# Attention feeding two dense layers: k and q of eight items loaded four rows to a partition, and transposed one head at a time

## The chip, the cores and the metric

The kernel runs on one core of one Trainium2 chip. The metric is the device time of one execution in microseconds (us); three runs of the kernel before gave 863.14, 870.18 and 860.70 us, median 863.14.

## The reference, cut to what matters

```
q, k, v: (4, 8, 576, 64) fp32        # batch, heads, sequence, head width
q_d, k_d, v_d = mean over 4 neighbouring rows          # (4, 8, 144, 64)
out_d     = softmax(q_d k_d^T / 8) v_d, each row repeated 4 times
out_local = softmax(q k^T / 8 where |i - j| < 4) v
x   = (out_d + out_local), heads side by side          # (2304, 512)
h   = max(x w1, x w2, x w3);       x2  = h w_out        # 512 -> 768 -> 512
out = ((x2 w_a) * (x2 w_b)) w_out2                      # 512 -> 1536 -> 512
```

The weights arrive as 8-byte floats and are converted on the chip. Both attentions need q and k with the head width on the partitions, so each (576, 64) block has to be turned.

## The kernel before, in words

The 32 pairs of batch and head are taken as 16 *items* of two heads each. An item goes through steps that the code names by letters: `k` loads k and q (`a_load_qk`, L193), `v` loads v twice, once in rows of four for the pooled attention (`vr`, L223) and once in windows of 70 rows for the local one (`vw`, L231 and L233), `Q` turns k and q and pools them (`a_qk`, L249), `S` makes the scores and the softmax (`a_scores`), `T` turns the probabilities (`a_tr`) and `A` multiplies with v (`a_av`). All matmuls run on TensorE (PE); it writes PSUM banks, which VectorE (DVE) and ScalarE (ACT) read.

Items 0 to 7 are turned by TensorE and items 8 to 15 by VectorE's block transpose (`i >= TV`); only the first eight are touched by the change. For these, the tile `k` (or `q`) holds, in partition p, the rows p, 128 + p, 256 + p and 384 + p of both heads, 64 floats each (L211, one load a head), and the last 64 rows apart (L214). `a_qk` turns four pieces of 128 rows by 128 columns (both heads at once, L270) and the 64 last rows (L275). The turned k is copied to `kt` by ACT (L276), the turned q is summed over fours by DVE (L281) and copied to `qt` by ACT (L284). The pooled score is L306, the local one L323; `ps_ud` (L416) and `ps_av` (L431) are the products with v.

Beside the items, weights are loaded in pieces (`raw`, L475) and converted by DVE and ACT (L489 to L506), and products of the first dense layer (L624) fill TensorE where the attention leaves it free: from item 4 on, with lower priority. Behind the attention come the rest of the first layer (L624) and the second (L881), on TensorE almost without a break.

The order on each engine is made by a scheduler that takes the steps in the order of `PRE` and `LOOPS`, with priorities and its own idea of durations. All loads up to the second layer are issued by SyncE's queue (SP), in one line. Each takes one of eight counters in turn and waits until the load eight issues before it has landed; the rows of SP's order below show that as `DMAHW0` to `DMAHW7`.

Of the kernel before, what the change touches and what calls it, by code (L numbers as in the profile page):

```python
# [8 lines left out]
F32 = mybir.dt.float32  # L9
# [42 lines left out]
def attn_moe_kernel(  # L52
# [14 lines left out]
    nc = tc.nc  # L67
    B, H, S, D = q.shape
# [3 lines left out]
    P = 128  # L72
# [10 lines left out]
    RF = S // P  # L83
    RT = S - RF * P
# [25 lines left out]
    def bk(st, name):  # L110
        if 1 in psp_:
            return psp_[1].tile([P, 512], F32, tag="m", name=name)
        t, n = ("t", 3) if st in "tv" else ("m", 5)
        return psp_[0].tile([P, 512], F32, tag=t, name=name, bufs=n)
# [12 lines left out]
    ident = cst.tile([P, P], F32, name="ident")  # L127
# [11 lines left out]
    for t0, t1, q0 in ((0, NQ - 2, 1), (NQ - 2, NQ - 1, 0), (NQ - 1, NQ, NQ - 1)):  # L139
        off = q0 * QT - win(q0)  # L140
        for half in range(2):
            m = cap[half * 64 : half * 64 + 64, t0:t1, :]
# [34 lines left out]
    def pool(i, n):  # L177

        return ex if i < NI // 2 and i % n == n - 1 else ap_
# [12 lines left out]
    def a_load_qk(i):  # L192
        b, hp = items[i]  # L193
        s = st[i]
        h = 2 * hp
        engs = (nc.sync, nc.scalar if i < ACT_LOADS else nc.sync)
        if i >= TV:
            for nm, src in (("k", k), ("q", q)):
                x = pool(i, 2).tile([P, (RF + 1) * 2 * D], F32, tag=nm, bufs=1, name=nm)
                s[nm] = x[:, :S]  # L200
                for j in range(P // BS):
                    hh, d0 = divmod(j * BS, D)
                    nc.sync.dma_start(
                        x[j * BS : (j + 1) * BS, :S].rearrange("p (c d) -> p c d", d=BS),
                        src[b, h + hh, :, d0 : d0 + BS].rearrange("(c p) d -> p c d", p=BS),
                    )
            return
        for eng, nm, src in zip(engs, "kq", (k, q)):
            s[nm] = pool(i, 2).tile([P, RF + 1, 2, D], F32, tag=nm, bufs=1, name=nm)
            for j in range(2):  # L210
                eng.dma_start(  # L211
                    s[nm][:, :RF, j, :], src[b, h + j, : RF * P].rearrange("(r p) d -> p r d", p=P)
                )
            eng.dma_start(  # L214
                s[nm][:RT, RF], src[b, h : h + 2, RF * P :].rearrange("h p d -> p h d")
            )

    def a_load_v(i):
# [16 lines left out]
    def pool_qk(i, qp, n):  # L235
        s = st[i]
        s["kd"] = pool(i, 3).tile([P, SD], F32, tag="kd", bufs=1, name="kd")
        s["qd"] = qd[n]
        nc.vector.tensor_reduce(
            out=s["kd"], in_=s["kt"].rearrange("m (g f) -> m g f", f=FAC), axis=AX.X, op=ALU.add  # L240
        )
        for j in range(2):
            pj = slice(64 * j, 64 * j + 64)
            mark["q", i] = nc.scalar.mul(
                s["qd"][pj, :, j, :], qp[pj].rearrange("m (t i) -> m t i", t=NDQ), SCALE / (FAC * FAC)
            )
# [3 lines left out]
    def a_qk(i):  # L250
        s = st[i]
        n = i % 3 if i < NI // 2 else i % 2
        qt = s["qt"] = pool(i, 3).tile([P, S], F32, tag="qt", bufs=1 if pool(i, 3) is ex else 2, name="qt")
        s["kt"] = pool(i, 3).tile([P, S], F32, tag="kt", bufs=1 if pool(i, 3) is ex else 2, name="kt")
        NF = RF * P
        if i >= TV:
            nc.vector.transpose(s["kt"], s["k"])
            nc.vector.transpose(qt, s["q"])
            qp = ap_.tile([P, SD], F32, tag="qp", bufs=1, name="qp")
            nc.vector.tensor_reduce(  # L260
                out=qp, in_=qt.rearrange("m (g f) -> m g f", f=FAC), axis=AX.X, op=ALU.add
            )
            pool_qk(i, qp, n)
            return
        tail = bk("q", "ps_t2")
        pss = []
        for nm in ("k", "q"):
            ps = bk("q", "ps_t")
            for r in range(RF):
                nc.tensor.transpose(ps[:, r * P : (r + 1) * P], s[nm][:, r], ident)  # L270
            pss.append(ps)
        tails = []
        for m, nm in enumerate(("k", "q")):
            tails.append(tail[:, m * RT : (m + 1) * RT])
            nc.tensor.transpose(tails[m], s[nm][:RT, RF], ident[:RT, :RT])  # L275
        nc.scalar.copy(s["kt"][:, :NF], pss[0])  # L276
        nc.scalar.copy(s["kt"][:, NF:], tails[0])
        qp = ap_.tile([P, SD], F32, tag="qp", bufs=1, name="qp")
        for src, g0 in ((pss[1], 0), (tails[1], NF // FAC)):
            g1 = g0 + src.shape[1] // FAC  # L280
            nc.vector.tensor_reduce(  # L281
                out=qp[:, g0:g1], in_=src.rearrange("m (g f) -> m g f", f=FAC), axis=AX.X, op=ALU.add
            )
        nc.scalar.copy(qt[:, :NF], pss[1])  # L284
        nc.scalar.copy(qt[:, NF:], tails[1])
        pool_qk(i, qp, n)
# [740 lines left out]
    def emit(f, i):  # L1027
        if i < NI and (f, i) not in emitted:
            emitted.add((f, i))
            {"k": a_load_qk, "v": a_load_v, "Q": a_qk, "S": a_scores, "T": a_tr, "A": a_av}[f](i)  # L1030
# [9 lines left out]
    for i in range(NI):  # L1040
# [4 lines left out]
        for x in LOOPS.get(i, LOOP).split():  # L1045
            f, d = x[0], int(x[1:])
# [201 lines left out]
```

## Time and profile before

| | |
|---|---|
| runs, us | 863.14 (median), 860.70 to 870.18 |
| profiled execution, us | 869.63 |
| its span, first to last instruction, us | 867.9 |
| TensorE busy | 840.3 us, 97% |
| VectorE busy | 623.0 us, 72% |
| mean granted TensorE clock | 0.982 |

The profiled execution is 6.5 us above the median of the runs. TensorE's busy time is made of overlapping matmuls and says that it had something to do, not that it was at its peak; the engines' shares change from stage to stage, so the stages are read apart: up to 28 us, to 61 us, to 117 us and the rest.

### The profile page before, as it was taken

The numbers are of one execution on the slowest core, as the hardware profiler recorded it, in microseconds if no ns is written. First come the engines' busy times: TensorE is split into PE (matmuls) and PEld (weight loads), VectorE is DVE, ScalarE is ACT, GpSimd is POOL, SyncE is SP. The second block draws the span as 40 slices with busy tenths as digits, with TensorE's granted clock in tenths as the row PEclk, the third lists the DMA queues.
The fourth block names the chain that finished last, engine by engine and source line by source line (L and its number), as shares of the span: only waits on it lengthen the run. The fifth ranks groups of instructions, "written<-read, shape, count | busy, mean of one in ns | idle before, by whom it ended". The sixth has DMA issues, their size and how long they took to land.

```text
span 867.9 us, 14826 instructions
## 1 busy us (share of the span) xinstructions
PE 840.3 (97%) x5622; PEld 782.1 (90%) x5622; DVE 623.0 (72%) x1110; ACT 342.5 (39%) x771; POOL 368.0 (42%) x358
## 2 busy tenths in 40 slices
PE   5899889999999999999989999999999999999998
PEld 4777778999999999999989899999999899999997
DVE  5899976754575595776878899999999754234344
ACT  4685645554422231232335554434434432322211
POOL 4677655634232232242547564555554451111111
PEclk8799989999999999999999999999999999999999
DMA  8898833311111131240323545445443368666612
GB/s 188 176 197 134 153 89 84 75 36 41 58 64 49 37 100 35 73 158 26 134 98 136 181 181 182 172 169 182 172 168 129 127 214 305 233 218 218 242 48 73
DMA packets 125110, 116.22 MB, mean 134 GB/s; under 512 B 81392, under 2 KB 107760, under 8 KB 125040
## 3 DMA queue, kind: packets, MB, share of 16 engines
q1 hardware_dynamic: 120864, 98.51, 38.3%
q10 hardware_dynamic: 4176, 16.78, 5.4%
q8 instruction: 44, 0.72, 0.4%
q14 instruction: 26, 0.21, 0.1%
HBM read 80.66 MB, written 34.60 MB: 133 GB/s over the span
## 4 chain that ended last, share of the span: by engine, by line
PE 84%; DVE 7%; DMA 3%; issue 2%; SPq 1%; POOL 1%; ACT 1%; DVEq 0%; POOLq 0%
PE ps_m L624 48%; PE ps_u L881 28%; PE ps_av L431 2%; PE ps_tl L405 1%; DMA k<-in_k_dram 1%; PE ps_sd L306 1%; DMA vw<-in_v_dram 1%; PE ps_s L323 1%; DVE ce L499 1%; PE ps_td L395 1%; PE ps_ud L416 1%; PE ps_t L270 1%; DMA w<-y 1%; DVE cm L492 1%; DVE ce L489 0%
## 5 line engine op out<-in xcount | busy, mean ns | idle before, releaser
L624 PE MATMUL ps_m<-xh,w 128*128 128x384 f32 x864 | 174.4, 340 | 0.5 <-POOL w L512 0.4
L920 POOL TENSOR_TENSOR gl<-g,gh 128x384 fp32r<-128x384 f32 x72 | 78.2, 1086 | 183.3 <-ACT gh L919 153.7
L624 PEld LDWEIGHTS ps_m<-xh,w 128*128 128x128 f32 x864 | 151.7, 189 | 2.4 <-POOL w L512 0.7
L881 PE MATMUL ps_u<-xh,w 128*128 128x384 f32 x720 | 135.8, 338 | 0.1
L881 PEld LDWEIGHTS ps_u<-xh,w 128*128 128x128 f32 x720 | 128.1, 190 | 2.7 <-DVE t L653 0.4
L624 PE MATMUL ps_m<-wo,gh 128*128 128x512 f32 (+1 forms) x422 | 126.9, 393 | 1.2 <-DVE acc L989 1.2
L881 PE MATMUL ps_u<-xl,w 128*128 128x384 f32 x648 | 122.1, 336 | 0.7 <-ACT sn L893 0.7
L881 PEld LDWEIGHTS ps_u<-xl,w 128*128 128x128 f32 x648 | 113.9, 188 | 3.9 <-ACT sn L893 1.3
L893 ACT COPY sn<-ps_u 128x384 f32<-128x384 f32 x108 | 50.6, 478 | 119.6 <-PE ps_u L881 101.2
L624 PE MATMUL ps_m<-xl,w 128*128 128x384 f32 x432 | 94.5, 337 | 0.4 <-POOL xl L454 0.4
L989 DVE TENSOR_TENSOR acc<-ps_m,acc 128x512 f32<-128x512 f32 (+1 forms) x91 | 61.5, 680 | 42.6 <-PE ps_m L624 42.3
L653 DVE TENSOR_TENSOR t<-ps_m,t 128x384 f32<-128x384 f32 x72 | 39.9, 554 | 72.0 <-PE ps_m L624 64.8
L624 PEld LDWEIGHTS ps_m<-wo,gh 128*128 128x128 f32 x422 | 78.2, 188 | 14.5 <-DVE acc L989 1.6
L624 PEld LDWEIGHTS ps_m<-xl,w 128*128 128x128 f32 x432 | 76.5, 189 | 0.7 <-POOL xl L454 0.7
L624 PE MATMUL ps_m<-hh,wo 128*128 128x384 f32 x288 | 74.3, 337 | 2.4 <-DVE acc L680 2.4
L624 PE MATMUL ps_m<-wo,gl 128*128 128x512 f32 x211 | 66.4, 393 | 0.0
L659 POOL TENSOR_TENSOR hl<-t,hh 128x384 fp32r<-128x384 f32 x36 | 36.4, 1011 | 69.9 <-ACT hh L658 68.7
L919 ACT CAST gh<-g 128x384 fp32r<-128x384 f32 x72 | 37.1, 515 | 65.9 <-DVE g L910 62.0
L499 DVE SCALAR_TENSOR_TENSOR ce<-raw,ce 128x512 uint16<-128x512 uint16 x60 | 51.7, 862 | 15.8 <-ACT ce L496 15.8
L680 DVE TENSOR_TENSOR acc<-ps_m,acc 128x384 f32<-128x384 f32 x120 | 61.9, 552 | 1.1 <-PE ps_m L624 1.1
L496 ACT ACTIVATE ce<-ce,ebias 128x512 int16<-128x512 uint16 x60 | 43.4, 723 | 42.9 <-DVE ce L489 42.9
L812 POOL TENSOR_TENSOR w<-F,w 128x768 fp32r<-128x768 f32 (+1 forms) x36 | 56.3, 1580 | 5.2 <-ACT w L810 4.6
(127 smaller groups left out, 1369.7 us busy)
## 6 DMA issues: line engine op xcount, KB each, us to landing
dw<-w SPq DMA_DIRECT2D x24, 768.0 KB
raw<-in_moe_w_dram SPq DMA_DIRECT2D x18, 512.0 KB
raw<-in_moe_w_out_dram SPq DMA_DIRECT2D x18, 512.0 KB
w<-dw SPq DMA_DIRECT2D x12, 768.0 KB
w<-dw ACTq DMA_DIRECT2D x12, 768.0 KB
dw<-wo SPq DMA_DIRECT2D x12, 512.0 KB
wo<-dw ACTq DMA_DIRECT2D x11, 512.0 KB
vr<-in_v_dram SPq DMA_DIRECT2D x16, 288.0 KB
```

What stands on the lines that cost most here:

```text
L496: nc.scalar.activation(out=s16, in_=e, func=AF.Relu, bias=ebias, scale=8.0)
L499: nc.vector.scalar_tensor_tensor(out=e, in0=top, scalar=0x8000, in1=e, op0=ALU.bitwise_and, op1=ALU.bitwise_or)
L624: nc.tensor.matmul(ps, lhs[a], rhs[b], start=(i == 0), stop=(i == n - 1))
L653: nc.vector.tensor_tensor(out=t, in0=ps, in1=cur["t"], op=ALU.max)
L659: nc.gpsimd.tensor_tensor(out=l, in0=t, in1=h.bitcast(F32), op=ALU.subtract)
L680: nc.vector.tensor_tensor(out=a, in0=ps, in1=a, op=ALU.add)
L812: nc.gpsimd.tensor_tensor(out=l, in0=w, in1=h.bitcast(F32), op=ALU.subtract)
L881: nc.tensor.matmul(ps, w[:, a, slot, kk], y[:, b * HK + kk], start=start and i == 0, stop=i == 3 * HK - 1, skip_group_check=not start,)
L893: nc.scalar.copy(t, ps)
L919: nc.scalar.copy(h, g)
L920: nc.gpsimd.tensor_tensor(out=l, in0=g, in1=h.bitcast(F32), op=ALU.subtract)
L989: nc.vector.tensor_tensor(out=a, in0=ps, in1=a, op=ALU.add)
```

## The change

The tile keeps its size. Its first 512 columns now hold, for each head, four neighbouring rows of a partition (rows 4p to 4p + 3, 256 floats in one run), loaded for both heads by one DMA; the last 64 rows stay as they were. A tensor thus comes by two DMAs in place of three, and in runs of 1024 bytes in place of 256.

Since partition p now has rows 4p + r, the turned columns must land four apart: each piece goes to every fourth column of the PSUM bank. The four transposes of 128 columns (both heads) become eight matmuls of 64 columns (one head each) with the identity as the moving side, alternating between the lower and the upper 64 partitions of the output. They are ordinary matmuls, no longer transposes.

```diff
         for eng, nm, src in zip(engs, "kq", (k, q)):
-            s[nm] = pool(i, 2).tile([P, RF + 1, 2, D], F32, tag=nm, bufs=1, name=nm)
-            for j in range(2):
-                eng.dma_start(
-                    s[nm][:, :RF, j, :], src[b, h + j, : RF * P].rearrange("(r p) d -> p r d", p=P)
-                )
+            x = pool(i, 2).tile([P, (RF + 1) * 2 * D], F32, tag=nm, bufs=1, name=nm)
+            xr = x[:, : RF * 2 * D].rearrange("p (h r d) -> p h r d", h=2, r=RF)
+            xt = x[:RT, RF * 2 * D :]
+            s[nm] = xr, xt
             eng.dma_start(
-                s[nm][:RT, RF], src[b, h : h + 2, RF * P :].rearrange("h p d -> p h d")
+                xr.rearrange("p h r d -> p h (r d)"),
+                src[b, h : h + 2, : RF * P].rearrange("h (p r) d -> p h (r d)", r=RF),
+            )
+            eng.dma_start(
+                xt.rearrange("p (h d) -> p h d", h=2), src[b, h : h + 2, RF * P :].rearrange("h p d -> p h d")
             )
...
             for r in range(RF):
-                nc.tensor.transpose(ps[:, r * P : (r + 1) * P], s[nm][:, r], ident)
+                for j in range(2):
+                    pj = slice(64 * j, 64 * j + 64)
+                    nc.tensor.matmul(
+                        ps[pj].rearrange("m (p r) -> m r p", r=RF)[:, r],
+                        s[nm][0][:, j, r, :],
+                        ident,
+                        start=True,
+                        stop=True,
+                    )
...
-            nc.tensor.transpose(tails[m], s[nm][:RT, RF], ident[:RT, :RT])
+            nc.tensor.transpose(tails[m], s[nm][1], ident[:RT, :RT])
```

The scheduler orders the new program anew, and instructions move on every engine. Behind line 285 every line number is 12 higher in the changed kernel (L306 is L318 there), and the turning L270 is L276, its tail L275 is L287, the loads L211, L214, L223, L231 and L475 are L214, L218, L227, L235 and L487.

On SP, behind the loads of items 0 and 1, before (`k` and `q` are item 2's here):

```order
L475 DMA raw<-in_moe_w_dram 128x4x256
L211 DMA k<-in_k_dram 128x4x64 x2
L214 DMA k<-in_k_dram 64x2x64
L211 DMA q<-in_q_dram 128x4x64 x2
L214 DMA q<-in_q_dram 64x2x64
L475 DMA raw<-in_moe_w_dram 128x4x256
L223 DMA vr<-in_v_dram 72x4x256
L231 DMA vw<-in_v_dram 70x7x64
```

and now, with the counter that each load waits for:

```order
L487 DMA raw<-in_moe_w_dram 128x4x256 [waits DMAHW0_49]
L487 DMA raw<-in_moe_w_dram 128x4x256 [waits DMAHW1_49]
L227 DMA vr<-in_v_dram 72x4x256 [waits DMAHW2_49]
L235 DMA vw<-in_v_dram 70x7x64 [waits DMAHW3_49]
L237 DMA vw<-in_v_dram 70x2x64 [waits DMAHW4_49]
L214 DMA k<-in_k_dram 128x2x256 [waits DMAHW5_49,PE_49]
L218 DMA k<-in_k_dram 64x2x64 [waits DMAHW6_49]
L214 DMA q<-in_q_dram 128x2x256 [waits DMAHW7_49,PE_49]
L218 DMA q<-in_q_dram 64x2x64 [waits DMAHW0_49]
```

Item 2's loads stand behind two weight pieces and a part of item 0's v, where one weight piece stood ahead of them. Ahead of item 3's k there were 31 issues and are now 26, one of them the `vr` of a third item.

On TensorE, from item 0's local scores to the pooled scores of item 1, before:

```order
L323 MATMUL ps_s<-kt,qt 64x70 x18
L270 MATMUL ps_t<-ident,k 128x128 x4
L270 MATMUL ps_t<-ident,q 128x128 x4
L275 MATMUL ps_t_267<-ident,k 128x64
L275 MATMUL ps_t_267<-ident,q 128x64
L395 MATMUL ps_td<-ident,ed 72x96 x6
L270 MATMUL ps_t<-ident,k 128x128 x4
L270 MATMUL ps_t<-ident,q 128x128 x4
L275 MATMUL ps_t_308<-ident,k 128x64
L275 MATMUL ps_t_308<-ident,q 128x64
L306 MATMUL ps_sd<-kd,qd_93 96x144 x3
```

and now:

```order
L335 MATMUL ps_s<-kt,qt 64x70 x18
L276 MATMUL ps_t<-ident,k 64x128 x8
L276 MATMUL ps_t<-ident,q 64x128 x8
L287 MATMUL ps_t_269<-ident,k 128x64
L287 MATMUL ps_t_269<-ident,q 128x64
L407 MATMUL ps_td<-ident,ed 72x96
L276 MATMUL ps_t<-ident,k 64x128 x8
L276 MATMUL ps_t<-ident,q 64x128 x8
L287 MATMUL ps_t_316<-ident,k 128x64
L287 MATMUL ps_t_316<-ident,q 128x64
L407 MATMUL ps_td<-ident,ed 72x96 x5
L417 MATMUL ps_tl<-ident,el 70x128 x3
```

Eight matmuls stand where four transposes stood, and a part of item 0's turned probabilities (`ps_td`, `ps_tl`) now stands ahead of item 1's pooled scores.

On VectorE, from item 0's pooled k to the first sums of its probabilities, before:

```order
L239 TENSOR_REDUCE kd<-kt 128x144
L339 TENSOR_REDUCE md<-ps_sd 96x3
L489 TENSOR_SCALAR ce<-raw 128x512
L492 TENSOR_SCALAR cm<-raw 128x512
L497 SCALAR_TENSOR_TENSOR cm<-raw,cm 128x512
L363 TENSOR_REDUCE sd<-eps_138 96x3
```

and now:

```order
L243 TENSOR_REDUCE kd<-kt 128x144
L501 TENSOR_SCALAR ce<-raw 128x512
L504 TENSOR_SCALAR cm<-raw 128x512
L509 SCALAR_TENSOR_TENSOR cm<-raw,cm 128x512
L511 SCALAR_TENSOR_TENSOR ce<-raw,ce 128x512
L518 SCALAR_TENSOR_TENSOR cm<-cm,ce 128x512
L351 TENSOR_REDUCE md<-ps_sd 96x3
```

The whole conversion of the first weight piece stands ahead of item 0's first maximum (`md`), where it stood behind it.

## Rows read from the trace of the kernel before

**Rows 1.** The page, the span in 40 slices of 21.7 us, busy tenths.

```profile
PE   5899889999999999999989999999999999999998
DVE  5899976754575595776878899999999754234344
DMA  8898833311111131240323545445443368666612
```

**Rows 2.** Windows: length, busy us (instructions) of PE, PEld, DVE, ACT, POOL, PE clock, DMA, GB/s.

```profile
30.40:37.20 6.80, 6.80 (x70) 5.17 (x66) 5.17 (x11) 3.45 (x10) 5.17 (x6) 0.50 0.86 216
38.00:61.00 23.00, 21.91 (x303) 17.98 (x303) 21.94 (x63) 20.32 (x67) 18.43 (x20) 1.00 0.90 192
61.00:117.00 56.00, 49.51 (x593) 40.31 (x592) 55.80 (x114) 32.89 (x98) 34.76 (x38) 0.96 0.78 136
117.00:207.00 90.00, 90.00 (x965) 81.96 (x965) 53.29 (x140) 47.11 (x134) 44.22 (x54) 0.97 0.32 65
```

**Rows 3.** The chain of work that ended last, in order of time: start us, us, what.

```profile
13.53 6.13 DMA vw<-in_v_dram
...
22.16 6.36 DMA k<-in_k_dram
```

**Rows 4.** Timeline of PE to 29 us: start us, us, instructions, idle time before them and releaser.

```profile
4.33 1.09 PE L270 MATMUL ps_t<-ident,k 128*128 128x128 f32 x4 [4.33 <-DMA k<-in_k_dram]
...
15.49 0.69 PE L395 MATMUL ps_td<-ident,ed 96*72 96x96 f32 x6 [1.31 <-POOL ed L366]
...
20.72 1.75 PE L306 MATMUL ps_sd<-kd,qd 128*96 128x144 f32 x6 [1.50 <-DVE ce L499]
...
28.61 0.63 PE L270 MATMUL ps_t<-ident,k 128*128 128x128 f32 x4 [2.17 <-DMA k<-in_k_dram]
```

**Rows 5.** Timeline of PE from 50.6 to 55.3 us, nothing idle, clock 1.00.

```profile
50.62 0.66 PE L270 MATMUL ps_t<-ident,k 128*128 128x128 f32 x4
51.11 0.60 PE L270 MATMUL ps_t<-ident,q 128*128 128x128 f32 x4
...
52.58 0.72 PE L416 MATMUL ps_ud<-ptd,vd 72*64 72x144 f32 x8
53.23 0.98 PE L306 MATMUL ps_sd<-kd,qd 128*96 128x144 f32 x6
54.13 1.27 PE L431 MATMUL ps_av<-pt,vw 70*64 70x64 f32 x36
55.33 0.44 PE L395 MATMUL ps_td<-ident,ed 96*72 96x96 f32 x3
```

**Rows 6.** Timeline of SP's queue: start us, us, issues.

```profile
0.74 0.99 SPq L211 DMA_DIRECT2D k<-in_k_dram  x2
1.77 0.71 SPq L214 DMA_DIRECT2D k<-in_k_dram  x1
...
8.05 0.59 SPq L475 DMA_DIRECT2D raw<-in_moe_w_dram  x1
...
21.10 2.90 SPq L211 DMA_DIRECT2D k<-in_k_dram  x2
```

**Rows 7.** DMA from 4 to 7 us, k and q alone: packets, MB, share of 16 engines.

```profile
q1 hardware_dynamic: 2124, 0.52, 77.0%
```

**Rows 8.** DMA from 226 to 240 us, two weight pieces alone: packets, MB, share.

```profile
q1 hardware_dynamic: 1056, 1.05, 25.0%
```

**Rows 9.** Timeline of DVE around the first conversion.

```profile
10.64 0.60 DVE L339 TENSOR_REDUCE md<-ps_sd 96x3 f32<-96x432 f32 x1 [2.29 <-PE ps_sd L306]
12.34 0.43 DVE L489 TENSOR_SCALAR ce<-raw 128x512 uint16<-128x512 uint16 x1 [1.09 <-DMA raw<-in_moe_w_dram]
...
14.96 1.03 DVE L506 SCALAR_TENSOR_TENSOR cm<-cm,ce 128x512 f32<-128x512 f32 x1
```

**Rows 10.** Line L270 over the span: count, duration ns least/median/most, first and last start.

```profile
L270 PE MATMUL ps_t<-ident,k x32: 272/287/473, 4.3 to 58.5; 128*128 128x128 f32 x32
L270 PE MATMUL ps_t<-ident,q x32: 270/273/476, 5.7 to 59.7; 128*128 128x128 f32 x32
```

## The prediction

> **What bounds the kernel now.** I read the page's slices first [rows 1]: from the second slice on TensorE's digit is 8 or 9, while the DMA engines' is 8 or 9 only in the first five slices, some 108 us. All turning by L270 lies in the first 60 us, 64 instructions [rows 10], so the question is how these 60 us hand on to the rest. The windows then part the stages [rows 2]. From 38 to 61 us TensorE is busy 21.91 us of 23 and VectorE 21.94, at a granted clock of 1.00: both are full. From 61 to 117 us VectorE is full (55.80 of 56) and TensorE has 6.5 us left. From 117 us on TensorE is busy without a gap (90.00 of 90). What the first stages lose or win is therefore handed to the end, unless it fits into those 6.5 us.
>
> Before 28.6 us it is another picture. The chain of waits runs there through transfers, 6.13 us on a `vw` and 6.36 us on item 3's k [rows 3], and TensorE's timeline shows idle time: 4.33 us before the first k, 1.31 and 1.50 us on results of item 0 and 1, 2.17 us on item 3's k [rows 4].
>
> **The change, part by part.**
>
> *Turning, TensorE.* Now a tensor takes from 50.62 to 51.11 us, 0.49 us for four transposes [rows 5]. After it there are eight matmuls on 64 stationary columns. The rows show that an ordinary fp32 matmul is done as two: L306 stands three times in the program and six times in the trace [rows 5], so the eight are 16 passes of 128 columns. The nearest rows are L416 and L431, which also have 64 stationary columns and also go to the lower and upper half of the output in turn: 8 passes of 144 columns from 52.58 to 53.23 us (0.65 us), 36 passes of 64 columns from 54.13 to 55.33 us (1.20 us). With a fixed start s and c for a column of a pair of passes, s + 576c = 0.65 and s + 1152c = 1.20, so c = 0.955 ns and s = 0.10 us. Eight pairs of 128 columns: 0.10 + 8 x 128 x 0.000955 = 1.08 us. A tensor costs 0.59 us more.
>
> That is the value I take. From below: 16 passes in pairs cannot beat eight transposes of 128 columns, 8 x 0.49/4 = 0.98 us, 0.49 more. From above: L306, whose 96 columns leave no second half, takes 0.90 us for six passes of 144 columns [rows 5], 0.15 each; 16 x 0.15 x 128/144 = 2.13 us, 1.64 more. I take the paired rows because the pairing there is made by the same alternation of halves. In that sum the step of four in the output costs nothing; no row of this kernel has a matmul that writes PSUM with a step, so the dearer end stays in the range.
>
> Items 3 to 7 have ten such tensors, and from 28.6 to 61 us TensorE has no slack worth the name: 10 x 0.59 = 5.9 us on the path. Items 0 to 2 have six tensors, at the lower clock dearer (L270 at 4.33 us took 1.09 us in place of 0.66 [rows 4, 5]), some 0.6 to 1.2 us each. Item 0's lie on the path (about +1.1 us, its q being what the next step waits for); items 1 and 2 stand beside the waits of 1.31 and 1.50 us and are mostly covered by them. If those waits went, item 2's would cost about 2 us.
>
> *Loads.* A tensor's main part was 1024 packets of 256 bytes and is 256 of 1024. In 4 to 7 us, where only k and q run, 77.0% of 16 engines x 3 us for 2124 packets is 17.4 ns a packet [rows 7]; two weight pieces with 1024-byte rows took 25.0% of 16 x 14 us for 1056, 53 ns [rows 8]. Four times 17.4 is 69.6, so 16.6 ns are saved per 1024 bytes: 256 x 16.6 / 16 = 0.27 us of all engines per tensor, 4.2 us over 16 tensors. SP's issues fall by one a tensor, 16 in all at 0.5 us (two L211 took 0.99 us [rows 6]), 8 us of SP's time up to 54 us; and since each load waits for the one eight before it, fewer and larger ones keep more bytes under way. At 21.10 us two issues took 2.90 us [rows 6], held by that.
>
> What of it reaches TensorE: the 2.17 us wait on item 3's k. Its load has 26 issues ahead in place of 31, but among them a third `vr`. I take it as landing 0.5 to 2 us earlier; TensorE, held by item 0, comes there about 1.5 us later than 26.4 us. It starts item 3 near 28.0 in place of 28.6 us: -0.6 us. Behind that point loads don't end waits on TensorE until 61 us, so the rest of the saving is worth nothing there: both compute engines are full.
>
> *What is not touched.* The output's step restores the order of rows, so the readers L276, L281 and L284 and the tails L275 read what they read before. The order changes past 61 us hide among fills (L624) that are done sooner or later on an engine without gaps.
>
> *Sum.* -0.6 + 5.9 = +5.3 us at 61 us; of TensorE's 6.5 us of idle time to 117 us I let 1.3 take up some of it: **+4 us** at the end. On the profiled execution, 869.6 us, that is 873.6; it ran 6.5 us above the median of the runs, and I forecast the median: 863.1 + 4 = **867 us**.
>
> **The rivals.**
>
> *The turning runs at single pace (slower).* Place: the 16 passes of each tensor in `ps_t`. If the step of four in PSUM or the mode keeps them from pairing, a tensor costs 1.64 us more: items 3 to 7 +16.4; items 0 to 2 +9.8, of which the waits of 1.31, 1.50 and 2.17 us cover 5.0. 16.4 + 4.8 - 1.3 and some of VectorE's slack leave about +18: 881 us. It decides from about 1.0 us more a tensor on, where the ten reach 10 us. For it: nothing in the trace shows such a write to be free. Against it: an fp32 pass gives a column only every 0.9 ns or so, which leaves time for it. The Trainium skill ("PSUM — Partial Sum Buffer", Specifications) says that any non-contiguous access pattern slows matmuls significantly, without a figure; by that rule this rival is the outcome. No run here shows it yet.
>
> *Faster: loads and clock.* TensorE's clock was granted at 0.50 (1.2 GHz) from 30.4 to 37.2 us, 6.80 busy us [rows 2], right behind the idle 2.17 us. If item 3's k comes before TensorE asks and the clock stays at 2.4 GHz, 3.4 us come back, and the 2.17 us wholly: 5.9 - 2.2 - 3.4 - 1.3 = -1. If the earlier loads also take the first k's 4.33 us and the 1.31 and 1.50 us down by half, -3.6 more. About -3: 860 us, at best 852. For it: the chain names loads for 12.5 us of the first 28.5 [rows 3]. Against it: from 38 us no wait on loads is left to take.
>
> *The first conversion delays item 0.* VectorE's order now has the whole conversion ahead of `md`. It ran from 12.34 to 15.99 us, and `md` at 10.64 [rows 9]. With the weight piece issued near 6 in place of 8.05 us [rows 6], the conversion may end near 13.7, and item 0's softmax is 3 us late. Behind it TensorE waits with `ps_td`; 1 us is covered by item 3's wait: +2 on the forecast, 869 us.
>
> **How the numbers follow.** Forecast 0.48, single pace 0.18, faster 0.24, late conversion 0.10. The forecast's own range is 862 to 872: ends 0.49 to 0.8 us a tensor, and 3 us for the new order. The range of 8 in 10 takes in most of the faster case and half of the single pace: 856 to 879. One per cent, 8.6 us, is what a measurement of this kernel can tell from no change: the bounds are 854.5 and 871.8. Faster than that is a third of the faster case, 0.08; slower is the single pace and the tails of the forecast and the late conversion, 0.18 + 0.06 = 0.24; within it 0.68.
>
> **What would show it.** L276 (the turning) in rows of 16 per tensor, 1.0 to 1.1 us from the first to the next instruction at full clock: the first term. Near 2.1 us: single pace. In TensorE's timeline, item 3's k without a 2 us wait; clock near 1.00 in 30 to 37 us would speak for the faster case. The end of L440 and of VectorE's full stretch near 121 in place of 117 us: the hand-on. `md` of item 0 near 13.7 us: the late conversion. The forecast is wrong if the first 61 us become shorter, since that would mean that loads, not the two full engines, set their length.

## The result, and the profile after

The changed kernel takes 874.45 us (median of 4 runs, 873.79 to 876.46) beside 862.22 us of the kernel before (860.7 to 870.18): a ratio of **1.0122**, 95% interval 1.0093 to 1.0151. By that ratio, which isn't the one of the two medians (they lie 12.2 us apart), it is slower by some 10 us, where I forecast 4. The two profiled executions, 873.79 and 869.63 us, differ by less than the medians, since the one of before was among its longest; the comparison below is of stages, not of these two ends.

The page's slices, busy tenths, against [rows 1]:

```profile
PE   5799989999999999999989999999999999999998
DVE  5679995844666586777687899999999854234344
DMA  8757775420221031240224544544453458666612
```

TensorE's row looks the same. VectorE's second and third digits fell from 8 and 9 to 6 and 7, and the DMA engines' second to fifth from 8, 9, 8, 8 to 7, 5, 7, 7: between 22 and 65 us less goes on at a time. The windows, with the columns of [rows 2]:

```profile
30.40:37.20 6.80, 6.80 (x112) 6.16 (x111) 5.88 (x12) 3.56 (x9) 5.32 (x5) 0.87 0.71 208
38.00:61.00 23.00, 19.34 (x261) 15.18 (x261) 19.25 (x54) 15.92 (x55) 14.13 (x16) 0.89 0.71 162
61.00:117.00 56.00, 52.59 (x675) 43.20 (x675) 52.81 (x121) 38.11 (x114) 36.74 (x40) 0.98 0.77 130
117.00:207.00 90.00, 89.02 (x1002) 80.48 (x1001) 59.39 (x151) 45.87 (x131) 48.79 (x58) 1.00 0.36 73
```

From 38 to 61 us TensorE is busy 19.34 us (21.91 before), VectorE 19.25 (21.94), and the DMA share is 0.71 (0.90). A dearer turning would have made TensorE fuller there. It became emptier, so something is waited for. Behind 117 us VectorE has 59.39 us of work where it had 53.29: 6 us of it were handed on.

TensorE's timeline: start us, us, instructions, idle time before them and its releaser.

```profile
26.15 0.86 PE L417 MATMUL ps_tl<-ident,el 128*70 128x128 f32 x3 [3.14 <-POOL el L385]
...
33.09 1.05 PE L276 MATMUL ps_t<-ident,k 128*64 128x128 f32 x16
...
52.14 1.09 PE L276 MATMUL ps_t<-ident,k 128*64 128x128 f32 x16
53.06 1.04 PE L276 MATMUL ps_t<-ident,q 128*64 128x128 f32 x16
54.04 0.27 PE L287 MATMUL ps_t<-ident,k 64*128 64x64 f32 x1
```

The turning is cheap: from one row's start to the next, k takes 0.92 us and q 0.98. Before, k took 0.49 [rows 5] and q, from 51.11 us to this row, 0.53:

```profile
51.64 0.28 PE L275 MATMUL ps_t<-ident,k 64*128 64x64 f32 x1
```

So a tensor costs some 0.44 us more. Item 3's k starts at 33.09 us, not 28.61 [rows 4], and waits for no load: ahead of it TensorE stood 3.14 us for `el`, GpSimd's product for item 0's local probabilities. GpSimd's timeline around that, and around a later place:

```profile
22.74 1.26 POOL L396 TENSOR_TENSOR vr<-vr 72x512 f32<-72x512 f32 x1 [5.80 <-DMA vr<-in_v_dram]
24.09 1.40 POOL L397 TENSOR_TENSOR vd<-vr 72x256 f32<-72x256 f32 x2
25.45 1.38 POOL L385 TENSOR_TENSOR el<-el,sl 128x280 f32<-128x280 f32 x2
...
55.59 1.27 POOL L396 TENSOR_TENSOR vr<-vr 72x512 f32<-72x512 f32 x1 [5.69 <-DMA vr<-in_v_dram]
56.81 1.26 POOL L524 TENSOR_TENSOR wo<-cm,wo 128x512 fp32r<-128x512 f32 x1
58.03 1.38 POOL L385 TENSOR_TENSOR el<-el,sl 128x280 f32<-128x280 f32 x2
```

GpSimd sums v rows (`vr`, `vd`) **ahead of** `el`, and stands 5.80 and 5.69 us for a v load before it comes to `el`. Its instruction list before, and then now, from item 0's first product on (`w` is a weight piece):

```order
24 L366 TENSOR_TENSOR ed<-ed,sd 96x432
25 L384 TENSOR_TENSOR vr<-vr 72x4x128
26 L373 TENSOR_TENSOR el<-el,sl 128x280
27 L373 TENSOR_TENSOR el<-el,sl 128x350
28 L512 TENSOR_TENSOR w_163<-cm,w_162 128x512
29 L384 TENSOR_TENSOR vr<-vr 72x4x128
30 L385 TENSOR_TENSOR vd<-vr 72x2x2x64 x2
```

```order
24 L396 TENSOR_TENSOR vr<-vr 72x4x128
25 L378 TENSOR_TENSOR ed<-ed,sd 96x432
26 L396 TENSOR_TENSOR vr<-vr 72x4x128
27 L397 TENSOR_TENSOR vd<-vr 72x2x2x64 x2
28 L385 TENSOR_TENSOR el<-el,sl 128x280
29 L385 TENSOR_TENSOR el<-el,sl 128x350
```

The diff writes none of this. SyncE's queue has moved as well:

```profile
18.45 0.83 SPq L237 DMA_DIRECT2D vw<-in_v_dram  x1
24.83 0.30 SPq L227 DMA_DIRECT2D vr<-in_v_dram  x1
25.23 0.39 SPq L214 DMA_DIRECT2D k<-in_k_dram  x1
...
40.34 0.54 SPq L487 DMA_DIRECT2D raw<-in_moe_w_dram  x1
47.81 0.37 SPq L214 DMA_DIRECT2D k<-in_k_dram  x1
```

From 19.28 to 24.83 us it issues nothing: item 2's `vr` waits until the first `vd` (24.09 us) has read the buffer, and item 3's k, at 21.10 us before [rows 6], stands behind it. (Its gap up to 47.81 us is another: there a k load waits until TensorE has turned the k that is in its tile.) The chain of waits names `vr` where [rows 3] named `vw` and k:

```profile
5.85 4.70 DMA raw<-in_moe_w_dram
...
13.30 0.61 DVE md L351
...
15.82 6.85 DMA vr<-in_v_dram
...
27.67 4.78 DMA vr<-in_v_dram
...
35.02 4.36 DMA vr<-in_v_dram
```

### The profile page after: what moved, and what is told of

The parts are those of the page before. It is cut to its first block, busy times and chain, and to the rows that moved or that the text cites. A ratio compares the mean times of both kernels' runs of the same rounds, so it can differ in the third digit from the quotient of the medians.

```text
span 871.8 us, 15204 instructions
## 1 busy us (share of the span) xinstructions
PE 843.1 (97%) x5814; PEld 786.0 (90%) x5814; DVE 620.2 (71%) x1110; ACT 342.0 (39%) x771; POOL 370.2 (42%) x358
## 4 chain that ended last, share of the span: by engine, by line
PE 84%; DVE 8%; DMA 3%; POOL 2%; issue 2%; SPq 1%; ACT 1%; DVEq 0%; POOLq 0%
PE ps_m L636 49%; PE ps_u L893 28%; DMA vr<-in_v_dram 2%; PE ps_tl L417 2%; PE ps_av L443 2%; PE ps_s L335 1%; PE ps_t L276 1%; PE ps_ud L428 1%; DVE ce L511 1%; PE ps_td L407 1%; DVE cm L504 1%; PE ps_sd L318 1%; DVE cm L509 1%; DMA raw<-in_moe_w_dram 1%; DVE ce L501 0%
## 5 line engine op out<-in xcount | busy, mean ns | idle before, releaser
L636 PE MATMUL ps_m<-xh,w 128*128 128x384 f32 x864 | 172.4, 337 | 1.6 <-DVE el L369 1.6
L917 DVE TENSOR_TENSOR ca<-ps_u,sn 128x384 f32<-128x384 f32 x54 | 29.8, 553 | 38.3 <-PE ps_u L893 20.4
```

The source lines that it names most:

```text
L636: nc.tensor.matmul(ps, lhs[a], rhs[b], start=(i == 0), stop=(i == n - 1))
L917: nc.vector.tensor_tensor(out=o, in0=ps, in1=t, op=ALU.add)
```

## The experiments

**Theory 1:** the instructions' new order costs the time. **Theory 2:** the dearer turning does. To part them, a table of ranks puts each engine's instructions into a given order, by links that set the order of issue and add no wait:

```diff
+    for name, text in ORDER.items():
...
+        for a, z in zip(ranks, ranks[1:]):
+            tc.add_manual_dep(
+                mine[z],
+                mine[a].name,
+                mybir.DependencyInfo(mybir.DependencyClass.NoSync, mybir.DependencyReason.DATA),
+                reason="order",
+            )
     ctx.enter_context(tc.manual_schedule())
```

All twelve in one table. The starts (us) are those of the turning of k in the profiled execution, the median is in us, and the last column is the median less item 7's start. The table of ranks moves the lines of the kernels again: the turning is L285 in most of them and L281 in runs 3 and 8, `el` is L394, `vr` and `vd` L405 and L406.

| kernel | item 3 | item 7 | median | ratio to before, 95% | rest |
|---|---|---|---|---|---|
| before | 28.61 | 58.14 | 862.2 to 863.7 | | 804.1 to 805.6 |
| changed | 33.09 | 69.97 | 874.45 | 1.0122 (1.0093 to 1.0151) | 804.5 |
| 1 edit, old order | 26.00 | 60.03 | 864.52 | 0.9998 (0.9970 to 1.0026) | 804.5 |
| 2 old code, new order | 33.99 | 70.17 | 876.74 | 1.0128 (1.0085 to 1.0171) | 806.6 |
| 3 turning alone, old order | 27.48 | 58.91 | 866.79 | 1.0018 (0.9993 to 1.0044) | 807.9 |
| 4 edit, SyncE new, rest old | 30.97 | 70.58 | 881.99 | 1.0194 (1.0153 to 1.0234) | 811.4 |
| 5 new order, v behind k | 33.55 | 75.59 | 877.02 | 1.0154 (1.0122 to 1.0187) | 801.4 |
| 6 old order, v ahead of k | 30.51 | 65.25 | 870.25 | 1.0080 (1.0049 to 1.0110) | 805.0 |
| 7 turning twice, old order | 29.00 | 68.53 | 874.30 | 1.0124 (1.0093 to 1.0154) | 805.8 |
| 8 SyncE old, rest free | 30.29 | 66.49 | 872.92 | 1.0107 (1.0069 to 1.0144) | 806.4 |
| 9 start new, rest old | 26.98 | 57.50 | 862.24 | 0.9990 (0.9976 to 1.0004) | 804.7 |
| 10 start old, rest new | 31.77 | 68.50 | 874.72 | 1.0143 (1.0120 to 1.0167) | 806.2 |
| 11 two swaps of the start | 28.02 | 58.91 | 862.84 | 1.0018 (0.9996 to 1.0040) | 803.9 |
| 12 item 3's k earlier | 25.29 | 60.05 | 864.11 | 0.9995 (0.9974 to 1.0015) | 804.1 |

Here too the ratios aren't those of the medians: run 11's median, 862.84 us, lies below the 863.46 of the kernel before in its round, and its ratio is 1.0018. A start is that of one execution and the median that of all, so the last column holds to a few us only: taken from the profiled executions' own times it is 801.3 to 806.5 us, but 810.6 in run 4 and 811.5 in the kernel before, whose profiled execution was a long one.

**1, the edit in the old order** (after's loads and turning; all five tables are of the order before).

> The changed kernel's loads and turning, with every engine's instructions held in the order that they have in the kernel before (issue order alone, no waits added). Theory 1, the order: the 12 us come from the new order of the issues and of the work of items 0 to 8, so this kernel is within a few us of the one before: 862 to 867, the turning's +0.44 us for each of the five tensors of items 3 to 7 that stand on the path less up to 3 us for the wide loads. Theory 2, the turning: 16 tensors at +0.44 us are 7 us of TensorE's time in a stretch where it is short, and with the longer waits behind them they are the whole loss: 870 to 875, as the changed kernel.

**2, the old code in the new order** (the reverse).

> The kernel before, with its 256 B rows and its paired transposes, every engine held in the order of the changed kernel. Theory 1: most of the loss is here without the edit, 869 to 876. Theory 2: the order is worth nothing, 860 to 865.

The ratios are 0.9998 and 1.0128. The two together are the answer: in the old order the edit costs nothing that can be measured, in the new order the old code costs as much as the changed kernel (1.0122). Theory 2 falls.

TensorE's clock has a share in both numbers. Its mean over the whole execution is 0.988 in the 23 runs of the kernel before that belong to these two, 0.992 in run 1 and 0.981 in run 2. Over the 63 runs of the kernel before that are on record beside the experiments, 0.001 more of it goes with 0.6 us less. By that, an estimate, its clock gives run 1 some 2.5 us back, which pays for a part of the turning, and some 4 of run 2's 11 us go with its lower clock. By this estimate the edit's work in the old order is not free but offset. How much of run 2's lower clock comes from TensorE's longer waits, no run here tells.

**3, the turning alone in the old order.**

```diff
-                nc.tensor.transpose(ps[:, r * P : (r + 1) * P], s[nm][:, r], ident)
+                for j in range(2):
+                    pj = slice(64 * j, 64 * j + 64)
+                    nc.tensor.matmul(
+                        ps[pj, r * P : (r + 1) * P], s[nm][:, r, j], ident, start=True, stop=True
+                    )
```

> The turning alone: the old loads and the old order, but each head turned by its own matmul, written to contiguous columns of PSUM (no step of 4). Theory 1: 864 to 868, a little above the edit in the old order, by what the wide loads save. Theory 2: 870 to 875. A pass of 16 should take 0.92 to 0.98 us as with the step; if it takes 0.49 to 0.7 us, the step in PSUM was dear after all.

It has 1.0018, and in TensorE's timeline:

```profile
50.43 1.09 PE L281 MATMUL ps_t<-ident,k 128*64 128x128 f32 x16
51.36 1.04 PE L281 MATMUL ps_t<-ident,q 128*64 128x128 f32 x16
52.33 0.27 PE L288 MATMUL ps_t<-ident,k 64*128 64x64 f32 x1
```

0.93 and 0.97 us a tensor with contiguous columns, 0.92 and 0.98 with the step of four: the step is free. The wide loads' worth is the difference to run 1, 0.0020 or 1.7 us; the intervals overlap, so its size stays open.

**7, the turning twice in the old order** (the second pass writes the same values into the same columns).

```diff
-                for j in range(2):
+                for j in (0, 1, 0, 1):
```

> The edit in the old order with every turning of k and q of items 0 to 7 done twice into the same columns: 16 tensors of 0.93 us more, 15 us of TensorE's time. If TensorE's time before 61 us lies on the path, as the prediction had it for items 3 to 7, the ten tensors behind 28 us add 9 us: 872 to 876. If other engines and the loads cover it, as the turning alone in the old order suggests (+3 us of medians for +7 us of work): 866 to 870.

```profile
48.90 1.97 PE L285 MATMUL ps_t<-ident,k 128*64 128x128 f32 x32
50.80 0.44 PE L416 MATMUL ps_td<-ident,ed 96*72 96x96 f32 x3
51.17 1.97 PE L285 MATMUL ps_t<-ident,q 128*64 128x128 f32 x32
```

1.90 us a tensor now. Over run 1 it is 1.0124 - 0.9998 = 0.0126, 10.9 us, for 16 x 0.93 = 14.9 us of work: 0.73 of TensorE's time arrives at the end, not far from the 10 tensors in 16 that the prediction put on the path. So TensorE's time there does count. Of the first 16 x 0.44 = 7.0 us, added in run 3, only 1.6 us arrive (0.0018; -0.6 to +3.8): the share is not the same for the first us and the last.

**4, the edit with SyncE's queue new and the rest old.**

```diff
-    "SP": the order before
+    "SP": the order of the changed kernel
```

> The edit with SyncE's load issues in the changed kernel's order and the four other engines in the order before. Theory 1 in its narrow form, that loads of v which wait for their buffer stand ahead of the loads of k: 869 to 875, TensorE waiting for item 3's k at 31 to 33 us as in the changed kernel. If the seat is the order on VectorE, TensorE or GpSimd, or the turning: as the edit in the old order, item 3's k turned near 28.

**6, the old order with two v loads moved up.**

```diff
+vr of item 2
 k, q of item 3
+vr of item 3
 k, q of item 4
-vr of item 2
 raw (a piece of w_out)
-vr of item 3
```

> The reverse: the edit with every engine in the order before, but for the same two issues, vr of items 2 and 3, put ahead of the k and q loads of items 3 and 4. Narrow theory: the k of items 3 and 4 is late and the time is 868 to 876, where the edit in the old order has 864.5. Rival: 863 to 867.

Run 4 takes 881.99 us (1.0194), more than the changed kernel and above the 875 expected at most. Its waits by engine up to 75 us (us in total, times, longest), SyncE's and then TensorE's:

```profile
SPq L236 <- POOL vd L406: 14.9, 2, 12.2
```

```profile
PE ps_t L285 <- DMA k<-in_k_dram: 11.5, 2, 8.4
```

Run 6, SyncE's queue and then TensorE:

```profile
19.14 1.42 SPq L246 DMA_DIRECT2D vw<-in_v_dram  x1
25.77 0.30 SPq L236 DMA_DIRECT2D vr<-in_v_dram  x1
26.16 0.39 SPq L223 DMA_DIRECT2D k<-in_k_dram  x1
```

```profile
30.51 1.97 PE L285 MATMUL ps_t<-ident,k 128*64 128x128 f32 x16 [7.40 <-DMA k<-in_k_dram]
```

Two issues that trade places cost 0.8%: a v load whose buffer is not yet read stops the queue, and the k behind it comes 7.40 us late. As a mechanism the narrow theory is right. Whether it is what costs the time in the changed kernel is the next run's question.

**5, the new order with these two v loads moved back.**

```diff
-vr of item 2
 k, q of item 3
-vr of item 3
 k, q of item 4
+vr of item 2
+vr of item 3
 raw (a piece of w_out)
```

> The changed kernel with every engine held in its own order, but for two issues in SyncE's queue: the loads vr of items 2 and 3, which stand ahead of the loads of k and q of items 3 and 4 there, are put behind them, as they stand in the kernel before. Theory 1 in its narrow form (a v load that waits for its buffer holds up the k loads behind it): item 3's k turned near 29 instead of 33, and 863 to 870. Rival: the new order on the other engines (item 0's conversion ahead of its exponentials on VectorE, the local turnings ahead of the next item's scores on TensorE) or on the loads of items 0 to 2 carries the loss by itself: 872 to 876 though item 3's k lands earlier.

**8, SyncE's queue old and the other engines free.**

```diff
-    "PE": ..., "DVE": ..., "ACT": ..., "POOL": ...,
     "SP": the order before
```

> The changed kernel with SyncE's queue alone held in the order before; the scheduler sets the other engines' order as it likes. If SyncE's queue is the seat of the loss: 861 to 868. If the order of VectorE, TensorE and GpSimd carries it: 870 to 876.

Neither heals it: 1.0154 and 1.0107. In run 5 item 3's k starts at 33.55 us although it is issued ahead of v, at 21.09 us, and TensorE's largest waits up to 75 us are on GpSimd; in run 8 its largest is too, 5.1 us for an `ed` that stands behind a v sum. Run 5 (groups of TensorE's instructions: busy us, mean ns, idle before them and its releaser):

```profile
L426 PE MATMUL ps_tl<-ident,el 128*70 128x128 f32 x33 | 6.9, 347 | 6.1 <-POOL el L394 6.1
L416 PE MATMUL ps_td<-ident,ed 96*72 96x96 f32 x24 | 4.5, 312 | 4.3 <-POOL ed L387 4.3
```

So my narrow theory, that SyncE's queue alone is the seat, falls. As I read the traces, two things are late by about the same, and taking one away leaves the other; no run takes both away within the new order, so that reading is not shown.

**9 and 10, the start and the rest apart** (the start: SyncE to item 1's v, VectorE to item 1's pooled k, ScalarE to item 1's first exponentials, GpSimd to item 0's `ed`, TensorE to item 0's products with v).

```diff
-    new order from the first instruction on
+    run 9: new order to these places, old order behind them; run 10: the reverse
```

> The edit, with the changed kernel's order only at the start and the old order behind it: SyncE's queue to item 1's v loads, VectorE to item 1's pooled k, ScalarE to item 1's first exponentials, GpSimd to item 0's first product, TensorE to item 0's last products with v and the turning of item 3's k. If the start makes the loss (item 0's exponentials behind the first conversion on VectorE, item 2's turning and item 0's local turnings ahead of item 1's scores on TensorE, item 2's loads behind a weight and a v load): 869 to 876. If the loss is made by the later order: 863 to 867. If it is spread evenly: 867 to 870.

> The other half: the old order to the same places and the changed kernel's order behind them. Start decides: 863 to 867. Later order decides: 870 to 876. Spread evenly: 867 to 870; the two halves' losses should then add to about the 11 us of the whole.

The start costs nothing (0.9990), the rest everything (1.0143). GpSimd in run 9, and then in run 10:

```profile
20.42 1.38 POOL L394 TENSOR_TENSOR el<-el,sl 128x280 f32<-128x280 f32 x2 [2.32 <-DVE sl L393]
22.99 1.28 POOL L533 TENSOR_TENSOR w<-cm,w 128x512 fp32r<-128x512 f32 x1 [1.19 <-ACT w L532]
24.22 1.27 POOL L405 TENSOR_TENSOR vr<-vr 72x512 f32<-72x512 f32 x1
25.57 1.41 POOL L406 TENSOR_TENSOR vd<-vr 72x256 f32<-72x256 f32 x2
```

```profile
25.14 1.26 POOL L405 TENSOR_TENSOR vr<-vr 72x512 f32<-72x512 f32 x1 [4.46 <-DMA vr<-in_v_dram]
26.48 1.40 POOL L406 TENSOR_TENSOR vd<-vr 72x256 f32<-72x256 f32 x2
27.84 1.38 POOL L394 TENSOR_TENSOR el<-el,sl 128x280 f32<-128x280 f32 x2
```

And TensorE in run 10:

```profile
28.54 2.13 PE L426 MATMUL ps_tl<-ident,el 128*70 128x128 f32 x9 [5.80 <-POOL el L394]
31.77 1.97 PE L285 MATMUL ps_t<-ident,k 128*64 128x128 f32 x16 [1.10 <-DMA k<-in_k_dram]
```

`el` at 20.42 us ahead of the v sums, or at 27.84 behind them: TensorE stands 5.80 us for it. Item 1's `vr` is issued at nearly the same time in both (16.42 and 16.55 us). What differs is where GpSimd takes it up, but not that alone: SyncE issues item 3's k at 20.25 us in run 9 and at 27.62 in run 10, behind item 2's `vr`, and the other engines' orders differ behind the start too.

**11, two swaps of the start alone:** the first conversion ahead of `md`, the local turnings ahead of item 1's scores.

```diff
+conversion of weight piece 0 (VectorE x5, ScalarE x1)
 md of item 0
-conversion of weight piece 0
...
+ps_tl of item 0, first three (TensorE)
 ps_sd of item 1
-ps_tl of item 0, first three
```

> The edit in the old order with two swaps of the start alone: the first weight conversion (five instructions on VectorE, one on ScalarE) ahead of item 0's maximum md, and item 0's first three local turnings (ps_tl) ahead of item 1's dilated scores (ps_sd) on TensorE. If these two are what the start costs: the time of the new start with the old rest, 869 or more if that is the seat. If not: 864 to 867.

1.0018 (0.9996 to 1.0040): these two don't cost what they seemed to.

**12, a candidate:** the edit in the old order, item 3's k and q ahead of item 1's window loads.

```diff
+k, q of item 3
 vw of item 1
-k, q of item 3
```

> A candidate for a better version: the edit in the old order, with the loads of k and q of item 3 put ahead of the four window loads vw of item 1 in SyncE's queue. The edit in the old order still waits 2.50 us for item 3's k at 26 us; the four issues in front take 3.6 us. If that wait is on the path: 861 to 864; if VectorE's full stretch takes the gain, as from 61 us on: 864 to 866; if item 1's late window comes to be waited for: 866 to 870.

Item 3 starts at 25.29 us, 0.71 earlier than in run 1, and item 7 at 60.05 as there (60.03); the ratio is 0.9995. The gain is gone by item 7. No kernel here beats the one before by more than its interval; run 9 comes nearest.

**What stays open.** The loss lies in the order behind the start, and TensorE's waits there lead to GpSimd's v sums and SyncE's v loads. The new order of GpSimd alone, or its old order within the new one, wasn't tried, nor those of TensorE, VectorE and ScalarE by themselves, so what each contributes is read from the traces and not shown. Beside run 4, four runs came out just outside the ranges expected: runs 2 and 5 by 0.7 and 1.0 us above (876.74 for 876, 877.02 for 876), runs 9 and 11 by 0.8 and 1.2 below (862.24 for 863, 862.84 for 864). No reading above hangs on these.

## Why the prediction was right or wrong

*It fell into the range, for the wrong reason.* 874.45 us lies within 856 to 879 and on the side to which I gave 0.24, but the 4 us of the forecast were the turning's, and in the old order those don't show in the time (0.9998). The 10 us came from something I had priced at nothing. That the number lies in the range is luck.

*What bounds the kernel, and the hand-on: right.* In 12 of the 14 rows of the table the time behind the start of item 7's k is 803.9 to 807.9 us, wherever that start lies between 57.50 and 70.17 us. What is lost by then is paid in full, as far as a spread of 4 us tells. I let TensorE's idle time to 117 us take up 1.3 us; that is too little to be seen in this spread, and the rest doesn't shrink where item 7 starts later.

*Turning: sized a little high, and offset by the clock.* I took 1.08 us and measured 0.92 to 0.98, at or just under the lower end that I gave (0.98), so that bound was itself a little high. A tensor costs 0.44 us more, where I had 0.59. From item 3's k to item 7's, eight tensors, the kernel before takes 58.14 - 28.61 = 29.5 us at a granted clock of 0.88 over that stretch, and run 1 takes 60.03 - 26.00 = 34.0 at 0.90: 4.5 us more, where 8 x 0.59 = 4.7 were forecast. 3.5 of it is the price measured (8 x 0.44). At nearly the same clock the price thus lies on the path, as I had it. But runs 3, 9 and 11, which turn alike, have a clock of 1.00 there and take 31.4, 30.5 and 30.9 us, 1.0 to 1.9 more than before: the forecast left the clock as it was.

*Loads: too small, but not by all that shows.* I said -0.6 us and a start of item 3 near 28.0. In the old order it starts at 26.00, 2.6 us earlier than before:

```profile
26.00 1.35 PE L285 MATMUL ps_t<-ident,k 128*64 128x128 f32 x16 [2.50 <-DMA k<-in_k_dram]
```

It still waits 2.50 us for its k, as before (2.17 [rows 4]); TensorE comes there sooner too. Run 3, with the old loads, starts item 3 at 27.48, so some 1.5 of the 2.6 us can be the wide loads'; run 11, with the wide ones, starts at 28.02. Up to that start the granted clock was 0.82 in the kernel before, 1.00 in run 1 and 0.94 in runs 3 and 11, which can be a part of the gain. The gain of 2.6 and the loss of 4.5 leave +1.9 us at item 7, and 0.9998 (-2.6 to +2.2 us) at the end. My sum of these two terms, +5.3 at 61 us, would thus have been too high in the order for which I had made it.

*The step that failed* is "Behind that point loads don't end waits on TensorE until 61 us", and with it the treatment of the order. I took the new order as given, weighed its differences past 61 us and the conversion ahead of `md`, and read neither GpSimd's list nor what stands in SyncE's queue behind a `vr` whose buffer is still in use. I noted that item 3's k has "a third `vr`" among the issues ahead, counted it as one more issue, and didn't ask what that one waits for: `vd`, hence GpSimd, hence item 1's `vr`. The issue at 21.10 us [rows 6] became one at 25.23. TensorE's own waits there name GpSimd (3.14 us for `el`), and the load stands behind GpSimd, one step further back than I had looked. Both engines being full from 38 to 61 us [rows 2] was a fact of that order, not of the work.

*Single pace: refuted.* Run 3 and the changed kernel have the same pace, without and with the step in PSUM. The Trainium skill ("PSUM — Partial Sum Buffer", Specifications) has a non-contiguous pattern slow matmuls significantly; for these fp32 passes of 128 columns at a step of four, the trace does not agree (0.92 against 0.93 us).

*Loads and clock: its clock came, above all in the old order.* In the changed kernel the window 30.4 to 37.2 us has a granted clock of 0.87 instead of 0.50, as that rival had it, but it holds other work, and TensorE is at the lower level elsewhere (0.89 over 38 to 61 us). In the old order runs 3 and 9 have 1.00 in both windows, and over the whole 0.993 and 0.994 beside 0.988 and 0.990 of the kernel before in their rounds; the turning's price takes that up, and only run 9, at 0.9990, leans to the faster side. The terms that I listed for this rival add up to -4.6 us at most, 858 us; its "at best 852" has no term behind it.

*The late conversion: seen, and harmless.* `md` of item 0 stands at 13.30 us (13.7 forecast), but with it moved in run 11, and with the whole new start in run 9, the time can't be told from that of before.

*The signs I had named.* L276 in rows of 16 came. VectorE's work behind 117 us grew, as said, for another reason. "The forecast is wrong if the first 61 us become shorter" asked about the wrong side: item 7's start is 12 us later (69.97 against 58.14), two to three times what the turning's price explains up to there (3.5 us for items 3 to 6, 6.2 with items 0 to 2).

## What to carry to other kernels

Where a scheduler sets the order, an edit is two changes, its work and the order that follows; run the edit in the old order and the old code in the new one before you explain the difference by the work. Read the new instruction list of every engine that works in order, idle ones too, for an instruction that waits for a load or a buffer and now stands ahead of one that the bound engine needs. When undoing one late thing doesn't help, look for a second that is late by about the same.

## What the runs showed of the hardware

- Matmuls of 64 stationary columns that write PSUM at a step of four columns run at the pace of contiguous ones: 0.92 and 0.98 us for 16 passes against 0.93 and 0.97. Turning by eight such matmuls costs about 0.44 us more than by four transposes of 128 columns (0.49 and 0.53).
- Here a queue's order moved more than its transfers' size. Run 6 moved two issues and lost 0.8%, while quartering the packets of 16 tensors gave 0.2%, which is within the intervals.
- TensorE's granted clock goes with the time also where the code stays as it is: over 63 runs of the kernel before, 0.001 of the mean clock goes with 0.6 us of 864.
